# Clustered attention and two MLPs on one core: the times that order its instructions are replaced

## The chip, the cores and the metric

The kernel runs on one core of a Trainium2 chip. The metric is the device time of one execution in microseconds (us). Of the kernel before, three runs were timed, and one more execution was profiled.

## The reference

Attention in which a query sees only the keys of its own cluster (batch 2, 8 heads, 768 tokens, head size 64, 16 centroids a head), then two MLPs on the 1536 tokens. All data is fp32.

```python
q_assign = argmax(einsum('bhsd,hcd->bhsc', q_n, c_n), axis=-1)   # q_n, k_n, c_n: rows divided by their norm
k_assign = argmax(einsum('bhsd,hcd->bhsc', k_n, c_n), axis=-1)
mask = q_assign[:, :, :, None] == k_assign[:, :, None, :]
scores = where(mask, q @ k.T / sqrt(D), -1e9)
attn = exp(scores - max(scores)); attn = attn / (sum(attn) + 1e-9)
x = (attn @ v)                       # to (1536 tokens, 512)
h = x @ w_in;  x = (h * cos(h)) @ w_out               # MLP 1, 512 -> 2048 -> 512
h = x @ w_in2; x = where(h > 0, h, exp(min(h, 0)) - 1) @ w_out2   # MLP 2
```

## The kernel before

**Arithmetic.** TensorE (PE) takes fp32 operands rounded to a shorter form. So each operand is split into a high part and a low part (value minus high part), and a product is made of two or three matmuls. Splitting is work for the other engines: ScalarE (ACT), VectorE (DVE) and GpSimd (POOL).

**Attention.** It handles the 16 heads of the batch in 8 pairs. Each pair has 12 steps, a step being 128 query rows of one head against all 768 keys; 96 steps in all. For a pair, the rows of q and k are transposed (raw_pe, in two halves each), split (raw_out, raw_copy, raw_low) and put together by six DMAs into the stacks X0, X1, T0, T1 (stack). The sums of squares give norms (square, sum_sq, seed, norm_step, norms). The products with the centroids (sims_pe, 12 matmuls for k and 12 for q; X0 serves the pair's first head, X1 its second) are added, scaled, and their first largest gives the cluster of a token (sims_add, sims_scale, sims_max, sims_eq, sims_first, best, assign). The result M is transposed (mask_pe) and copied by mask_out as extra rows into T0 and T1, so that a matmul of the T stacks puts the mask into the scores. The first pair is set up by functions of its own (first_pe, first_hi, first_low, first_hi2), for each of its heads (j = 0, 1) apart.

A step is: qk (L741 with the X stacks, L744 with the T stacks), rowmax (DVE, L749), expo (ACT, L757, the exponential), turn (PE, L766, six transposes in two halves), p_hi (ACT, L780) and p_lo (DVE, L786). Three steps are a half, for which av (L797) makes 12 matmuls with the values; two halves are a unit, one head of one batch. A unit's denominators are turned into reciprocals (recip), written to DRAM and read back spread over the partitions (recip_rows, recip_out: the DMAs row<-den and R<-row), and multiplied in by POOL (x_add, x_mul).

**MLPs.** Each MLP m has 3 tiles t of 512 tokens, and for each tile 16 parts f of the inner dimension. For each (m, t, f), g1 (L198) makes 12 matmuls, act in eight parts applies the nonlinearity and splits the result into GH and GL, and g2 (L257) makes 12 more that add into four accumulators. Before a tile, x_hi and x_lo split its tokens into XH and XL (four pairs); after it, finish copies the accumulators out (e = 0 to 3), in MLP 2 to the output by DMA. The weights of a part f come in two DMAs of 512 KB (load_w), and are converted by w_part: 0 on ACT (L133), 1 and 2 on DVE (L135, L137), 4 on ACT (L142), 5 on POOL (L148); 3 does nothing. They stay in their slot for the three tiles. open_mlp issues the loads of the first ten parts of MLP 1, and close_attention, after the last product of attention, opens the memory for the others and issues their loads.

**Order.** All of this is written out as a list of items, each with a time; the list is sorted by time and then issued, so the times give nothing but the order in which each engine, and each DMA queue, gets its instructions. Every engine works off its instructions in that order and waits where data or a buffer isn't there. The times come from seven tables: FIRST (the first pair, j = 0 and j = 1), PAIR (the other pairs; time 0 of pair pp is step 12(pp-1)), STEP (each step), HALF, UNIT, LAST (the end of attention and the start of MLP 1, counted from step 96) and MLP (m = 0, 1; counted for each unit from step 96 + 2.147). One unit of time is one attention step, or one MLP part.

```python
for n in range(NS):
    for name, time in STEP.items():
        fn, own = named(name)
        at(n + time, fn, n, *own)
...
    for time, _, part, args in sorted(items, key=lambda a: a[:2]):
        part(*args)
```

Buffers that matter here: two PSUM buffers for scores, three for transposes and similarities, one for the attention's output; two buffers u for weights in conversion.

Of the kernel before, what the change touches and what calls it, by code (L numbers as in the profile page):

```python
# [54 lines left out]
def kernel(ctx: ExitStack, tc: tile.TileContext, q, k, v, centroids,  # L55
# [225 lines left out]
    with ExitStack() as actx:  # L281
# [726 lines left out]
```

## Time and profile before

| | |
|---|---|
| timed runs, median | 811.31 us |
| lowest and highest of three | 810.27, 811.99 us |
| span of the profiled execution | 806.6 us |
| PE busy | 781.8 us |
| DVE, ACT, POOL busy | 469.1, 490.3, 408.3 us |

The span runs from the first to the last instruction of the profiled execution; this execution has no time of its own, so the span stands beside the median of the timed runs, 4.7 us above it, and what lies around the span is in that difference. "Granted clock" is the share of full speed that TensorE's clock had in a stretch: 1.00 is 2.4 GHz, 0.50 is 1.2 GHz.

### The profile page before, as it was taken

The page shows a single profiled execution, that of the slowest core. Times are in us where ns is not written, and L with a number is a line of the kernel's source. Part 1 is how long each engine was busy: PE and PEld are TensorE (multiplying, and loading weights), DVE is VectorE, ACT ScalarE, POOL GpSimd, SP SyncE. Part 2 cuts the span into 40 slices and gives each one's busy share as a digit, 9 for nine tenths or more (in the row PEclk, how much of TensorE's full clock was granted, in tenths as well). Part 3 has the DMA queues.
Part 4 walks back from the last instruction along what each step waited for, and adds up shares of the span by engine and source line. Part 5 has one row for each costly group of instructions (what it writes and reads, how often), then busy time and mean ns, then how long its engine had stood idle before and what let it go on. Part 6 is the DMA issues. An engine that isn't in the chain of part 4 may idle for free.

```text
span 806.6 us, 11273 instructions
## 1 busy us (share of the span) xinstructions
PE 781.8 (97%) x4003; PEld 668.4 (83%) x4003; DVE 469.1 (58%) x751; ACT 490.3 (61%) x894; POOL 408.3 (51%) x426
## 2 busy tenths in 40 slices
PE   4999999999998998999999999999999999999997
PEld 3899999999997776888888888888888888888886
DVE  7899899899899768863432443577774111121110
ACT  3798998998999966654433453566563433343332
POOL 3657667667655777652221132379997221122221
PEclk7799999999999999999999999999999999999999
DMA  3645746746637394000000045571000100010001
GB/s 100 141 102 124 181 97 134 167 99 148 161 73 245 52 380 162 1 0 1 1 1 0 1 156 198 176 253 52 1 1 1 52 1 1 0 40 14 0 1 52
DMA packets 62920, 67.99 MB, mean 84 GB/s; under 512 B 30416, under 2 KB 51408, under 8 KB 62864
## 3 DMA queue, kind: packets, MB, share of 16 engines
q1 hardware_dynamic: 62864, 67.28, 30.2%
q8 instruction: 31, 0.51, 0.3%
q14 instruction: 25, 0.20, 0.1%
HBM read 46.17 MB, written 3.19 MB: 61 GB/s over the span
## 4 chain that ended last, share of the span: by engine, by line
PE 82%; DVE 8%; ACT 3%; DMA 3%; POOL 1%; issue 1%; SPq 0%; ACTq 0%; DVEq 0%; POOLq 0%
PE a L257 30%; PE h L198 29%; PE pt L766 6%; PE px L797 6%; PE s L741 3%; PE s L744 3%; PE pt_sim L581 2%; DVE m L749 2%; DMA raw<-in_moe_w_out_dram 2%; PE pt_raw L437 1%; DVE PL L786 1%; POOL slot L148 1%; ACT u L133 1%; DVE u L137 1%; DVE M L647 1%
## 5 line engine op out<-in xcount | busy, mean ns | idle before, releaser
L240 POOL TENSOR_TENSOR GL<-A,GH 128x512 fp32r<-128x512 f32 x96 | 132.1, 1376 | 273.4 <-ACT GH L235 269.4
L198 PE MATMUL h<-XH,slot 128*128 128x512 f32 x768 | 251.9, 391 | 4.4 <-POOL slot L148 4.2
L198 PEld LDWEIGHTS h<-XH,slot 128*128 128x128 f32 x768 | 144.7, 189 | 36.1 <-POOL slot L148 5.6
L198 PE MATMUL h<-XL,slot 128*128 128x512 f32 x384 | 150.1, 391 | 0.0
L232 DVE SCALAR_TENSOR_TENSOR A<-R,h 128x512 f32<-128x512 f32 x48 | 33.0, 687 | 161.3 <-ACT R L230 151.0
L257 PE MATMUL a<-GH,slot 128*128 128x512 f32 x384 | 124.9, 389 | 0.0
L257 PE MATMUL a<-slot,GH 128*128 128x512 f32 x384 | 118.3, 389 | 0.0
L786 DVE TENSOR_TENSOR PL<-pt,PH 128x384 fp32r<-128x384 f32 x192 | 98.3, 543 | 19.4 <-ACT PH L780 17.8
L235 ACT ACTIVATE GH<-A 128x512 fp32r<-128x512 f32 x80 | 50.5, 632 | 76.5 <-DVE A L226 43.1
L780 ACT ACTIVATE PH<-pt 128x384 fp32r<-128x384 f32 x192 | 86.0, 495 | 11.4 <-PE pt L766 9.8
L749 DVE TENSOR_REDUCE m<-s 128x1 f32<-128x768 f32 x96 | 91.0, 948 | 3.1 <-PE s L744 1.8
L766 PE MATMUL pt<-ident,P 128*128 128x128 f32 x576 | 89.5, 280 | 1.4 <-DVE PL L786 1.2
L757 ACT ACTIVATE P<-s,m 128x768 f32<-128x768 f32 x96 | 87.2, 908 | 3.5 <-DVE m L749 3.1
L148 POOL TENSOR_TENSOR slot<-u,slot 128x1024 fp32r<-128x1024 f32 x32 | 79.7, 2492 | 12.8 <-ACT slot L142 12.6
L198 PEld LDWEIGHTS h<-XL,slot 128*128 128x128 f32 x384 | 72.4, 189 | 15.0
L257 PEld LDWEIGHTS a<-slot,GH 128*128 128x128 f32 x384 | 72.1, 188 | 15.0
L257 PEld LDWEIGHTS a<-GH,slot 128*128 128x128 f32 x384 | 72.0, 188 | 15.0
L766 PEld LDWEIGHTS pt<-ident,P 128*128 128x128 f32 x576 | 66.9, 141 | 12.6 <-DVE PL L786 6.4
L257 PE MATMUL a<-GL,slot 128*128 128x512 f32 x192 | 74.7, 389 | 0.0
L257 PE MATMUL a<-slot,GL 128*128 128x512 f32 x192 | 74.7, 389 | 0.0
L219 DVE SCALAR_TENSOR_TENSOR R<-A,h 128x512 f32<-128x512 f32 x48 | 32.9, 686 | 68.4 <-ACT A L215 68.4
L228 ACT ACTIVATE R<-h 128x512 f32<-128x512 f32 x48 | 28.5, 595 | 66.0 <-PE h L198 65.2
(139 smaller groups left out, 1276.9 us busy)
## 6 DMA issues: line engine op xcount, KB each, us to landing
raw<-in_moe_w_in_dram SPq DMA_DIRECT2D x32, 512.0 KB, 5.4
raw<-in_moe_w_out_dram SPq DMA_DIRECT2D x32, 512.0 KB, 6.5
nat_k<-in_k_dram SPq DMA_DIRECT2D x16, 192.0 KB, 4.3
nat_q<-in_q_dram SPq DMA_DIRECT2D x16, 192.0 KB, 3.9
nat_v<-in_v_dram SPq DMA_DIRECT2D x8, 384.0 KB, 3.6
R<-row SPq DMA_DIRECT2D x32, 96.0 KB, 3.4
out_dram<-o SPq DMA_DIRECT2D x12, 256.0 KB, 2.0
X0k<-hi SPq DMA_DIRECT2D x7, 192.0 KB, 2.6
```

The costliest lines, as they stand in the source:

```text
L148: eng.tensor_tensor(out=lo, in0=f32(w_u[m, f]), in1=f32(hi), op=ALU.subtract)
L198: nc.tensor.matmul(h, lhsT=a[:, kd, :], rhs=b, start=(kd == 0 and i == 0), stop=(kd == NKD - 1 and i == 2))
L232: nc.vector.scalar_tensor_tensor(out=A, in0=R, scalar=-1.0, in1=h, op0=ALU.add, op1=ALU.max)
L235: nc.scalar.activation(out=GH, in_=A, func=AF.Copy)
L240: eng.tensor_tensor(out=GL, in0=A, in1=f32(GH), op=ALU.subtract)
L257: nc.tensor.matmul(accs[m, t][e], lhsT=a, rhs=b, start=(f == 0 and i == 0), stop=(f == NF - 1 and i == 2))
L749: nc.vector.tensor_reduce(out=m, in_=st[n]["s"][:, :, 0:HW], axis=AX.XY, op=ALU.max, negate=True)
L757: nc.scalar.activation(out=P, in_=st[n]["s"][:, :, 0:HW], func=AF.Exp, bias=st[n]["m"], accum_out=dens[u][:, j, r:r + 1])
L766: nc.tensor.transpose(pt[:, c * 128:(c + 1) * 128], st[n]["P"][:, e, c * 128:(c + 1) * 128], ident)
L780: nc.scalar.activation(out=ph, in_=pt, func=AF.Copy)
L786: nc.vector.tensor_tensor(out=pl, in0=pt, in1=f32(ph), op=ALU.subtract)
L797: nc.tensor.matmul(tx[g][:, 0:HW], lhsT=V2s[pp][:, j, c, :], rhs=halves[g][a][:, c, :], start=(n == 0), stop=(n == 2 * C - 1))
```

## The change

The seven tables get other numbers. No function, no instruction, no buffer and no choice of engine is changed, and BASE stays 2.147; each engine has the same instructions in another order. The full tables are some 450 numbers; the entries that bear on the order around the opening, the keys' similarities, the av products, the change-over to the MLP and the ends of the tiles are these.

```diff
-FIRST = ({... 'mask_pe': -4.01798, 'mask_out:k': -1.754631, 'mask_out:q': -2.715055},
-  {'first_hi:k': -6.163385, 'first_hi2:k': -4.095755, 'first_low:k': -3.88111, 'first_low:q': -1.740567, 'first_hi2:q': -0.204062,
-   'sims_pe:k': -1.308999, 'sims_pe:q': 0.268773, 'sims_add:k': 0.722591, 'sims_scale': 1.092376, 'assign': 3.113711, 'mask_pe': 3.346959 ...})
+FIRST = ({... 'mask_pe': -7.3245, 'mask_out:k': -4.618, 'mask_out:q': -1.344},
+  {'first_hi:k': -27.1265, 'first_hi2:k': -26.4955, 'first_low:k': -26.5849, 'first_low:q': -39.3125, 'first_hi2:q': -45.6012,
+   'sims_pe:k': -11.2298, 'sims_pe:q': -11.089, 'sims_add:k': -5.6567, 'sims_scale': -4.7338, 'assign': 0.0315, 'mask_pe': 0.3042 ...})
...
-PAIR = {... 'raw_pe:k:1': 0.025604, 'stack:k': 1.900208, 'stack:q': 3.6443, 'load_nat:q': 1.096009, 'load_nat:v': -1.887999,
-  'sims_pe:k:7': 3.547059, 'sims_pe:k:6': 3.591015, ... 'sims_pe:k:5': 4.175453 ...}
+PAIR = {... 'raw_pe:k:1': 0.2089, 'stack:k': 2.1453, 'stack:q': 5.1167, 'load_nat:q': -2.0847, 'load_nat:v': 2.1455,
+  'sims_pe:k:1': 3.133, 'sims_pe:k:8': 3.1663, ... 'sims_pe:k:11': 5.282 ...}
...
-STEP = {'qk': -0.554281, 'rowmax': 0.318128, 'expo': 1.03429, 'turn:0': 1.783177, 'p_hi:0': 2.226495, 'p_lo:0': 2.784921, ...}
+STEP = {'qk': -0.2199, 'rowmax': 0.274, 'expo': 1.1941, 'turn:0': 2.2429, 'p_hi:0': 2.556, 'p_lo:0': 2.7986, ...}
-HALF = {'av:0:0': 5.403758, ... 'av:2:1': 4.964283, ...}
+HALF = {'av:0:0': 5.4843, ... 'av:2:1': 7.6553, ...}
-UNIT = {... 'recip_rows': 7.427179, 'x_mul': 13.848315}
+UNIT = {... 'recip_rows': 8.0355, 'x_mul': 15.1918}
-LAST = {'open_mlp': (-10.431815,), ...
-  'g1': (-0.307886, 1.731051, 4.372541, 5.094428), 'act:3': (6.073842, ..., 8.863032), 'g2': (6.668914, 8.520482, 9.303291, 9.815031),
-  'w_part:5': (5.381259, 5.610103, 6.550675, 6.924254, 7.503784, 8.022706),
-  'w_part:7': (9.14231, 9.347017, 9.526266, 9.904052, 10.071843, 10.148753), ...}
+LAST = {'open_mlp': (-12.9648,), ...
+  'g1': (0.1691, 2.4243, 3.6755, 4.8629), 'act:3': (5.6602, ..., 8.5703), 'g2': (7.6343, 9.1684, 9.5095, 9.8494),
+  'w_part:5': (5.543, 5.6643, 5.7277, 6.1291, 6.3037, 7.7047),
+  'w_part:7': (6.9143, 7.2499, 7.6194, 7.9283, 8.6967, 9.1755), ...}
...
-MLP = ({'g1': 1.795143, 'g2': 5.151129, 'late_g2:13': -0.690981, 'late_g2:14': -1.391747, 'late_g2:15': -0.882423 ...},
-  {'g1': 0.285498, 'g2': 4.282268, 'finish:0': 4.212529, 'finish:1': 4.739817, 'finish:2': 5.863002, 'finish:3': 5.213858 ...})
+MLP = ({'g1': 1.3754, 'g2': 4.3988, 'late_g2:13': -0.2473, 'late_g2:14': 0.1408, 'late_g2:15': -0.1717 ...},
+  {'g1': 0.168, 'g2': 4.6275, 'finish:0': 4.753, 'finish:1': 5.2414, 'finish:2': 5.2833, 'finish:3': 6.8395 ...})
```

PE's order in the change-over, read off the sorted lists: before g1(3), g2(0), g1(4), g2(1), g1(5), g2(2), g2(3), g1(6), g1(7), g2(4), g1(8); after g1(3), g1(4), g2(0), g1(5), g2(1), g2(2), g1(6), g2(3), g1(7), g2(4), g1(8).

## Rows read from the trace of the kernel before

**Rows 1.** The page: busy lines, and the chain that ended last by engine.
```profile
PE 781.8 (97%) x4003; PEld 668.4 (83%) x4003; DVE 469.1 (58%) x751; ACT 490.3 (61%) x894; POOL 408.3 (51%) x426
...
PE 82%; DVE 8%; ACT 3%; DMA 3%; POOL 1%; issue 1%; SPq 0%; ACTq 0%; DVEq 0%; POOLq 0%
```

**Rows 2.** Windows by stage: stretch, its length, busy us (instructions), granted clock, DMA share, GB/s.
```profile
0.00:40.00 40.00, 28.12 (x155) 24.91 (x155) 31.21 (x81) 23.12 (x44) 20.38 (x58) 0.79 0.49 119
40.00:225.00 185.00, 184.25 (x1268) 170.38 (x1267) 166.13 (x321) 169.82 (x387) 126.22 (x196) 1.00 0.60 135
225.00:278.00 53.00, 49.62 (x305) 44.47 (x306) 49.05 (x85) 50.32 (x101) 30.73 (x25) 1.00 0.43 120
278.00:315.00 37.00, 32.69 (x135) 25.91 (x135) 25.00 (x30) 25.44 (x34) 28.27 (x16) 0.95 0.93 316
315.00:802.30 487.30, 487.10 (x2148) 402.69 (x2146) 197.66 (x238) 220.55 (x331) 202.68 (x132) 1.00 0.12 40
```
The busy columns are PE, PE's weight loads, DVE, ACT, POOL.

**Rows 3.** The chain, in order of time: start us, us, what.
```profile
70.58 1.02 PE pt_sim L581 x10
...
101.27 1.02 PE pt_sim L581 x10
...
356.16 8.16 PE a L257 x36
```

**Rows 4.** Timeline of DVE, opening: start, us, line, operation, tiles [idle before].
```profile
17.99 0.36 DVE L647 TENSOR_TENSOR M<-desc,best 128x192 bf16<-128x192 f32 x1
18.38 0.95 DVE L511 SCALAR_TENSOR_TENSOR X1k<-s_raw,T1k 64x768 fp32r<-64x768 f32 x1
...
22.46 0.96 DVE L749 TENSOR_REDUCE m<-s 128x1 f32<-128x768 f32 x1 [1.19 <-PE s L744]
```

**Rows 5.** Timeline of PE, opening.
```profile
11.42 1.46 PE L581 MATMUL pt_sim<-CC,X0k 128*128 128x32 f32 x6 [2.21 <-ACT X0k L518]
...
18.40 0.82 PE L655 MATMUL pt_mask<-identb,M 128*128 128x128 bf16 x6 [2.91 <-DVE M L647]
```

**Rows 6.** Windows of the instructions on tile sm: DVE, POOL, clock, DMA.
```profile
22.00:32.00 10.00, 3.95 (x7) 0.00 (x0) 0.68 0.48 118
```

**Rows 7.** Windows of 2 us, all engines; columns as in rows 2.
```profile
26.00:28.00 2.00, 2.00 (x10) 1.90 (x10) 1.97 (x4) 0.64 (x1) 1.92 (x3) 0.50 0.18 41
28.00:30.00 2.00, 1.46 (x9) 1.14 (x8) 1.97 (x4) 1.87 (x6) 1.59 (x3) 0.90 0.94 230
...
308.00:310.00 2.00, 1.99 (x5) 1.62 (x6) 1.97 (x3) 2.00 (x3) 2.00 (x2) 0.58 1.07 369
```

**Rows 8.** Timeline of PE, the last pair's setup.
```profile
208.44 0.55 PE L437 MATMUL pt_raw<-ident,nat_k 128*128 128x128 f32 x3
...
217.09 0.47 PE L581 MATMUL pt_sim<-CC,X1k 128*128 128x32 f32 x3
```

**Rows 9.** Timeline of SP's DMA queue, the last pair's setup: time of issue.
```profile
212.17 0.59 SPq L477 DMA_DIRECT2D X1k<-lo  x1
```

**Rows 10.** Tile X1k between 190 and 225: its two DMAs.
```profile
DMA to landing us min/median/max: 3.0/3.9/4.8
```

**Rows 11.** Timeline of PE, change-over to the MLP.
```profile
278.00 0.39 PE L198 MATMUL h<-XH,slot 128*128 128x512 f32 x1
...
294.00 0.72 PE L198 MATMUL h<-XH,slot 128*128 128x512 f32 x2 [1.76 <-POOL slot L148]
...
308.01 0.99 PE L198 MATMUL h<-XH,slot 128*128 128x512 f32 x2 [2.39 <-POOL slot L148]
...
314.75 0.39 PE L198 MATMUL h<-XH,slot 128*128 128x512 f32 x1
```

**Rows 12.** Timeline of all engines, 284 to 294: the conversions of part 5.
```profile
284.73 1.13 ACT L133 ACTIVATE u<-raw 128x1024 f32<-128x1024 f32 x1 [0.94 <-DMA raw<-in_moe_w_out_dram]
...
291.22 2.72 POOL L148 TENSOR_TENSOR slot<-u,slot 128x1024 fp32r<-128x1024 f32 x1
```

**Rows 13.** Timeline of ACT, the end.
```profile
802.27 1.08 ACT L274 ACTIVATE o<-a 128x512 f32<-128x512 f32 x2 [0.71 <-PE a L257]
```

More of the change, by code (lines that the diff above doesn't have):

```diff
@@ L28 @@
-STEP = {'qk': -0.554281, 'rowmax': 0.318128, 'expo': 1.03429, 'turn:0': 1.783177, 'p_hi:0': 2.226495, 'p_lo:0': 2.784921, 'turn:1': 1.918261, 'p_hi:1': 2.322276, 'p_lo:1': 2.867829}
-HALF = {'av:0:0': 5.403758, 'av:0:1': 6.750175, 'av:1:0': 7.350891, 'av:1:1': 6.901501, 'av:2:0': 5.134225, 'av:2:1': 4.964283, 'av:3:0': 5.242615, 'av:3:1': 5.420227, 'av:4:0': 7.325687, 'av:4:1': 7.204538, 'av:5:0': 6.486225, 'av:5:1': 5.404756, 'x_main': 7.995152, 'x_low': 7.577939}
-UNIT = {'den_eps': 3.395449, 'recip': 4.382076, 'recip_rows': 7.427179, 'recip_out': 8.211055, 'x_add': 9.795484, 'x_mul': 13.848315}
@@ new lines @@
+PAIR = {'raw_pe:k:0': -0.743, 'raw_out:k:0': -0.2045, 'raw_low:k:0': 0.6817, 'raw_pe:k:1': 0.2089, 'raw_out:k:1': 0.4515, 'raw_low:k:1': 0.6139, 'stack:k': 2.1453, 'raw_pe:q:0': 1.5546, 'raw_out:q:0': 1.7927, 'raw_low:q:0': 3.1418, 'raw_pe:q:1': 2.3762, 'raw_out:q:1': 3.0458, 'raw_low:q:1': 4.0128, 'stack:q': 5.1167, 'square:k': 1.3021, 'square:q': 1.3101, 'sum_sq:k': 3.1266, 'sum_sq:q': 3.5134, 'sims_add:k': 5.7012, 'seed': 4.0682, 'sims_add:q': 7.1365, 'norms': 6.4333, 'sims_scale': 7.5265, 'sims_max': 7.7243, 'sims_first': 8.322, 'load_nat:k': -9.4917, 'load_nat:q': -2.0847, 'load_nat:v': 2.1455, 'raw_copy:k:0': -0.1846, 'raw_copy:k:1': -0.967, 'raw_copy:q:0': 1.7891, 'raw_copy:q:1': 3.107, 'best': 8.3585, 'sims_eq': 7.8239, 'values_hi:0': 5.6735, 'values_lo:0': 6.6448, 'values_hi:1': 9.3594, 'values_lo:1': 9.4649, 'norm_step:0': 4.1104, 'norm_step:1': 5.1523, 'norm_step:2': 6.1592, 'norm_step:3': 6.3018, 'sims_pe:k:0': 3.1708, 'sims_pe:k:1': 3.133, 'sims_pe:k:2': 5.0754, 'sims_pe:k:3': 3.3276, 'sims_pe:k:4': 3.491, 'sims_pe:k:5': 4.5188, 'sims_pe:k:6': 3.2098, 'sims_pe:k:7': 3.2376, 'sims_pe:k:8': 3.1663, 'sims_pe:k:9': 3.7707, 'sims_pe:k:10': 3.9263, 'sims_pe:k:11': 5.282, 'sims_pe:q:0': 6.7398, 'sims_pe:q:1': 6.6346, 'sims_pe:q:2': 6.079, 'sims_pe:q:3': 6.0556, 'sims_pe:q:4': 6.4121, 'sims_pe:q:5': 6.2837, 'sims_pe:q:6': 6.4203, 'sims_pe:q:7': 6.4759, 'sims_pe:q:8': 6.474, 'sims_pe:q:9': 6.435, 'sims_pe:q:10': 6.6393, 'sims_pe:q:11': 6.7459, 'assign': 8.771, 'mask_pe': 9.0336, 'mask_out': 9.3553}
@@ new lines @@
+STEP = {'qk': -0.2199, 'rowmax': 0.274, 'expo': 1.1941, 'turn:0': 2.2429, 'p_hi:0': 2.556, 'p_lo:0': 2.7986, 'turn:1': 2.3257, 'p_hi:1': 2.6658, 'p_lo:1': 2.8786}
+HALF = {'av:0:0': 5.4843, 'av:0:1': 5.5958, 'av:1:0': 5.4825, 'av:1:1': 7.7439, 'av:2:0': 7.6152, 'av:2:1': 7.6553, 'av:3:0': 6.8609, 'av:3:1': 6.0871, 'av:4:0': 5.5957, 'av:4:1': 7.241, 'av:5:0': 7.2689, 'av:5:1': 5.6122, 'x_main': 7.873, 'x_low': 7.8732}
+UNIT = {'den_eps': 4.4246, 'recip': 4.4277, 'recip_rows': 8.0355, 'recip_out': 8.2123, 'x_add': 12.5024, 'x_mul': 15.1918}
```

7 lines of the change are left out of this document (3 added, 4 removed).

## The prediction

> **What bounds the kernel now.** I read the page's busy lines and its chain first, then the span cut into stages, then each stage by its own timeline. TensorE (PE) is busy 781.8 of 806.6 us, and 82% of the chain that ended last is PE; VectorE (DVE), ScalarE (ACT) and GpSimd (POOL) lie between 51% and 61% [rows 1]. The change leaves every matmul in place, so only PE's 24.8 us of idle time, and the time in which its clock is low, can move. The stages say where that is [rows 2]: 11.9 us in the first 40 us, 0.75 in 185 us of steady attention, 3.4 in the last eighth of attention (225 to 278), 4.3 in the change-over to the MLP (278 to 315), 0.2 in the 487 us after it, and the 4.3 that are left lie behind the last matmul.
>
> Steady attention repeats every 30.69 us (101.27 less 70.58), which is 12 steps of 2.557 us, and the MLP's 12 matmuls of one g1 or g2 take 2.72 us (8.16 for 36) without a gap [rows 3]. Nothing can be gained there; something can be lost, because a matmul that comes up before its data stops PE at once. Gain can come from the opening, the change-over and the tail alone.
>
> **The opening.** Before assigns head 0, starts qk(0), and puts head 1's assignment between the first steps. After puts head 1's splits and similarities ahead of head 0's mask, and head 1's whole assignment ahead of the first row maximum. On DVE three splits of 0.95 us (X1k, and X1q twice) now stand in front of head 0's chain, which ended at 18.35 [rows 4]: 21.2 now. On PE mask_pe(0) is queued behind the sims of both tensors of head 1, up to 1.46 us each at the low clock [rows 5], which can't start before X1k is split. I get mask_pe at about 22.05 against 18.40. From mask_pe to the first row maximum the way is the same but for one of those sims, which stood before qk(0) and no longer does; the row maximum, at 22.46 in before [rows 4], starts some 3.2 us later.
>
> What is given back is head 1's chain, which ran between the row maxima while DVE was full (1.97 of 2 us in both windows of [rows 7]): 3.95 us on the tile of similarities [rows 6] and 0.36 for M [rows 4], 4.3 us. So DVE would be 1.1 us ahead at the sixth row maximum, if it stays the limit. Against that stands the clock. It fell to 0.50 (1.2 GHz) in the 2.21 us in which PE waited for X0k [rows 5], and was back at full (2.4 GHz) between 28 and 30 (0.90 over that window, so at about 28.4 [rows 7]), after PE had run without a gap from 18.40. In after PE waits some 5 us before head 1's sims, and its gapless run starts with mask_pe, 3.65 us later. If the return is as much later, 3.65 us more run at half rate and cost 1.8. Sum: +3.2 - 4.3 + 1.8 = **+0.7 us**. Bounds: -1.1 (the clock costs nothing), +5.0 (nothing is given back).
>
> The Trainium skill, page TensorE: Matmul & The Clock Gate, section Part 1: The HAM clock gate, says that the warm-up is a budget of time and not a number of matmuls. By it the half-rate stretch moves with the late start, and the opening is +0.7; if the return stayed at 28.4 it would be -1.1. The trace agrees in so far as the clock fell in a gap and rose within a dense run.
>
> **Steady attention.** On the three busy engines the step's own parts (qk two ahead, row maximum, exponential, turn, hi and lo copies) keep their order against each other; the av products of a half are dealt 5/1/6 to three steps instead of 6/0/6, which costs PE nothing. The sims of the keys come earlier. Their tables stand 3.55 - 0.03 = 3.52 steps behind raw_pe(k,1) in before and 3.13 - 0.21 = 2.92 in after. In the trace that was 217.09 - 208.44 = 8.65 us [rows 8], so now 7.2. The data of X1k goes by DMA: its last part is issued 3.73 us behind raw_pe [rows 9] and lands 3.0 to 4.8 us later [rows 10], so it is there 6.7 to 8.5 us behind raw_pe. The first X1k chunk comes some 0.3 us into the sims. The slack is then +0.8 to -1.0 us, where before had 0.1 or more. PE idles 0.12 us in a period (0.75 in six [rows 2]), so a wait isn't hidden by anything. Taking most pairs near the short landing I put **+0.5** for all; bounds 0 and +6 (1.0 in six pairs). The later stack and loads of q have more than a step of room.
>
> **End of attention.** The first ten weight DMAs are issued 1 us sooner, as one pair of denominator DMAs no longer stands before them; as many conversions as before stand ahead of step 96 on ACT, which is the limit there in both orders (50.3 of 53 us busy, DVE 49.1 [rows 2]): **0**. Bounds -1.1 and +1.1, one first conversion (1.13 us [rows 12]) in a better or worse place.
>
> **The change-over.** From g1(2) at 278.00 to g1(8) at 314.75 PE does 11 groups of 12 matmuls, 29.9 us by 2.72; it took 36.75, so 6.8 us are lost [rows 11]: 2.1 in g1(5), which waits 1.76 us for POOL's last conversion w5(5), and most of the rest in g1(7), 2.39 us of waiting for w5(7) and then matmuls at a granted clock of 0.58 [rows 7]. After moves the conversions of units 6 and 7 on ACT and DVE forward against the activations of units 3 to 5, so w5(6) and w5(7) go ahead; but it also takes one g2 out from before g1(5), which comes up 2.72 us earlier, at 288.9. Its third matmul (289.35) needs w5(5). That chain of five conversions started at 284.73 with the landing and ended at 293.94 [rows 12]: 9.2 us, of which 6.8 are work (the first 1.13, the last 2.72, 2.97 between them) and the rest waits. The last reciprocal comes some 0.4 us earlier, so the landing is at 284.3 and the end between 291.1 and 293.5. After has fewer items between the five, so I take 291.7, nearer the work alone. The stall is then 2.4 us, which is that of 308.01, and what followed that one was the slow stretch: ten matmuls took 3.98 us (308.01 to 311.99) where ten take 2.27, 1.7 lost. Unit 6's w5 then ends about 296.5 and is due about 299.5, unit 7's about 300.3 against 304.9: a w5 of 2.7 and a GL of 1.3 take POOL 4 us a unit and PE takes 5.44, so no second stall. Loss 2.4 + 1.7 = 4.1 in place of 6.8: **-2.7**. Bounds: with the end at 291.1 and the clock kept, as it was behind the 1.76 us (the matmuls after it were not longer), a loss of 1.8 and -5.0; with the end at 293.5 and the slow stretch, 4.2 + 1.7 and -0.9; with a second stall like the first, +1.2.
>
> **MLP and tail.** Where a tile of tokens changes, three g2 (8.16 us [rows 3]) cover the splits XH and XL; after leaves two in MLP 1 (5.44) and one in MLP 2 (2.72). Walking the splits by their durations I find the last XL of MLP 1 ready 6.4 to 7.6 us after the accumulators' end where it is needed at 7.7, and the tightest XL of MLP 2 at 3.9 against 4.3. **+0.2**, bounds 0 and +1.5. In the tail two output copies, 1.08 us together [rows 13], follow the last matmul, because the third output is queued behind the fourth; after has them in order, so one copy goes: **-0.5**, bounds 0 and -0.5.
>
> **Sum.** 0.7 + 0.5 + 0 - 2.7 + 0.2 - 0.5 = -1.8 us: a span of 804.8 for 806.6. The median of the three timed runs, 811.31, is 4.7 above this span, and I carry that over: **809.5 us**.
>
> **Rivals.**
> 1. *The late opening isn't made up* (slower). Place: the first row maximum. If ACT or the stack DMAs, and not DVE, hold the steps that follow, head 1's 4.3 us give nothing back and +5.0 stands for +0.7: 813.8. For it: ACT was 1.87 of 2 us busy at 28 to 30 [rows 7] and has the same work left. Against: DVE was fuller. It decides from an opening that is 4.1 us late (0.7, the 1.8 of gain, and 1.6 to be seen).
> 2. *The change-over gains almost nothing.* The chain of w5(5) keeps its 9.2 us and stops PE sooner instead of later: -0.9 for -2.7, 811.3.
> 3. *The keys' sims wait for their DMA* in each pair, 1.0 us in six: +6 for +0.5, 815.0. For it: PE has no idle time to hide it; against: landings of 4.8 us are the longest.
> 4. *The splits at the tile changes come late*, 1.0 us at each of five: +5 for +0.2, 814.3.
>
> **Chances.** Forecast 0.50, rivals 0.20, 0.16, 0.09 and 0.05. A measurement can tell about 0.2% (1.6 us) from no change. The forecast's own range is 805.5 to 811; of its half 0.44 lies over 1.6 us faster (a change-over without the slow stretch, 807.8, adds to it) and 0.06 within. Rival 2 gives 0.14 within and 0.02 slower, rival 1 0.03 and 0.17; 3 and 4 are slower. Faster 0.44, same 0.23, slower 0.33. The range runs from the forecast's lower end to a little over rival 1: 805.0 to 814.5.
>
> **What would show it.** Opening: the first row maximum at about 25.6, full clock at about 32, and the period marks of [rows 3] 0.7 us later. Steady: a period of 30.69 to 30.8; a wait of pt_sim on the DMAs of X1k would be rival 3. Change-over: one stall, at g1(5), of 2 to 2.5 us, none at g1(7). Tile changes: no gap. Tail: one copy behind the last matmul. The prediction is wrong if the marks come 3 us late, or if g1(6) or g1(7) stalls again.

## The result, and the profile after

After took 815.92 us in the median of seven runs (812.45 to 820.9), before 810.87 (810.11 to 811.99): a ratio of 1.0061, 95% interval 1.0034 to 1.0088. The change made the kernel 5 us slower, where 809.5 and "faster" were forecast, and the median lies outside the forecast range of 805.0 to 814.5; rival 3 had stood at 815.0. The runs of after also lie 8.5 us apart, those of before 1.9. The profiled execution of after took 813.07 us with a span of 811.3, so it is one of its quicker ones, and 1.8 us lie around the span. One execution in this document, the profiled one of the reverse experiment (848.65 us), is slow against the others of its kernel and stands in no median.

The page of after, busy lines and chain, as in [rows 1]:

```profile
PE 779.9 (96%) x4003; PEld 668.2 (82%) x4003; DVE 496.8 (61%) x751; ACT 487.4 (60%) x894; POOL 411.0 (51%) x426
...
PE 72%; DVE 11%; ACT 7%; DMA 5%; POOL 2%; issue 2%; SPq 1%; ACTq 0%; POOLq 0%; DVEq 0%
```

DMA went from 3% to 5% of the chain and PE from 82% to 72%. The same windows as in [rows 2], columns as there:

```profile
0.00:40.00 40.00, 26.30 (x141) 23.09 (x142) 28.83 (x80) 23.05 (x41) 19.94 (x56) 0.74 0.53 124
40.00:225.00 185.00, 177.72 (x1228) 165.18 (x1227) 161.44 (x310) 164.97 (x375) 121.41 (x183) 1.00 0.56 127
225.00:278.00 53.00, 50.58 (x328) 45.99 (x326) 49.75 (x88) 50.64 (x107) 31.84 (x39) 1.00 0.50 140
278.00:315.00 37.00, 33.20 (x143) 27.55 (x143) 29.08 (x36) 27.92 (x38) 25.14 (x14) 0.95 0.83 271
```

PE's idle time between 40 and 225 us was 0.75 us and is 7.3. A fixed window holds other work in a kernel that runs late, so the ledger is made from marks: the start of the n-th row maximum (DVE, L749) in each timeline. The columns after the first are us behind before at the same row maximum, called the lag below; "loads moved" and "FIRST alone" are experiments of the next section.

| row maximum of step | before, start | after | loads moved | FIRST alone |
|---|---|---|---|---|
| 0 | 22.46 | +3.55 | +3.38 | +3.50 |
| 12 | 54.60 | +1.46 | +1.29 | +1.59 |
| 48 | 146.66 | +5.21 | +0.38 | +1.91 |
| 84 | 238.28 | +7.25 | +0.37 | +1.67 |

The last matmul ended at 802.25 in before and at 807.51 in after (+5.3), the span at 806.6 and 811.3 (+4.7). So the opening cost 1.5 us, steady attention 5.8 (7.25 less 1.46), the rest won back 2.0 up to the last matmul and 0.6 behind it.

What PE waited for in after between 40 and 240 us (releaser: us in total, times, longest):

```profile
PE pt_mask L655 <- DVE M L647: 2.3, 7, 0.7
PE pt_sim L581 <- DMA X1k<-lo: 2.0, 2, 1.4
PE pt_sim L581 <- DMA X1q<-lo: 1.7, 4, 0.5
PE pt_sim L581 <- DMA X0q<-lo: 1.2, 2, 0.7
```

4.9 us are similarities that wait for DMAs of a stack, 2.9 of them for the stack of q, and 2.3 are the mask's transposes. None of these lines was there in before between 40 and 240. The chain of after runs through the same DMAs; the period, which was 30.69 us [rows 3], is 33.2 here (106.50 less 73.29), in the longest of the six periods:

```profile
67.89 5.26 DMA X1q<-lo
73.29 1.03 PE pt_sim L581 x8
92.46 4.17 DMA X1k<-lo
...
101.11 5.26 DMA X1q<-lo
106.50 1.04 PE pt_sim L581 x8
```

The timeline of the DMA queue, one pair later, shows what is new: the loads of v and k, with the denominators' DMAs between and behind them, now stand between the stack of k and the stack of q. In before both loads came after the stack of q or with the mask's DMAs.

```profile
93.78 0.62 SPq L479 DMA_DIRECT2D T1k<-hi  x1
94.45 0.59 SPq L311 DMA_DIRECT2D nat_v<-in_v_dram  x1
95.09 1.31 SPq L823 DMA_DIRECT2D R<-row  x2
96.44 1.29 SPq L317 DMA_DIRECT2D nat_k<-in_k_dram  x2
97.83 1.33 SPq L817 DMA_DIRECT2D row<-den  x2
99.26 0.51 SPq L474 DMA_DIRECT2D X0q<-hi  x1
```

Opening. PE waited 5.64 us before head 1's similarities and reached mask_pe at 22.00 (22.05 was forecast, 18.40 in [rows 5]):

```profile
19.41 1.46 PE L581 MATMUL pt_sim<-CC,X1k 128*128 128x32 f32 x6 [5.64 <-ACT X1k L518]
...
22.00 0.82 PE L655 MATMUL pt_mask<-identb,M 128*128 128x128 bf16 x6
```

The first row maximum started at 26.01 (25.6 was forecast). The granted clock was 0.65 over 30 to 32 us, so full from about 31.4 (28.4 in before [rows 7]):

```profile
30.00:32.00 2.00, 2.00 (x11) 1.67 (x10) 0.96 (x1) 1.95 (x6) 1.92 (x3) 0.65 1.00 257
```

End of attention. A new stall: on DVE the conversion L137 of weight part 3 (3.28 us beside POOL's L148) stands ahead of a split PL, and PE's turn waits 2.35 us for it. Timelines of DVE and of PE, then windows:

```profile
276.73 3.28 DVE L137 SCALAR_TENSOR_TENSOR u<-raw,u 128x1024 uint32<-128x1024 uint32 x1
279.93 1.01 DVE L786 TENSOR_TENSOR PL<-pt,PH 128x384 fp32r<-128x384 f32 x2
```

```profile
280.53 0.90 PE L766 MATMUL pt<-ident,P 128*128 128x128 f32 x3 [2.35 <-DVE PL L786]
...
300.83 0.72 PE L198 MATMUL h<-XH,slot 128*128 128x512 f32 x2 [1.45 <-POOL slot L148]
...
320.57 0.73 PE L198 MATMUL h<-XH,slot 128*128 128x512 f32 x2 [0.39 <-POOL slot L148]
```

```profile
280.00:282.00 2.00, 1.47 (x6) 1.47 (x7) 1.97 (x7) 1.90 (x4) 0.76 (x1) 0.64 0.04 8
282.00:284.00 2.00, 2.00 (x7) 1.61 (x6) 2.00 (x4) 1.96 (x3) 1.63 (x1) 0.51 0.08 2
```

Behind this wait the granted clock fell to 0.51, as it did to 0.58 behind the 2.39 us of [rows 11]. The change-over itself has two stalls left, 1.45 us at g1(5) and 0.39 at g1(8). From the last av at 290.59 to g1(8) at 319.57 PE does 10 groups of 12 matmuls, 27.2 us of work in 28.98: 1.8 us lost, where before lost 6.8 up to the same place; 2.5 with the 0.7 that g1(8) itself loses. Tail: all four copies run in order, and one of 0.6 us is left behind the last matmul (ACT; two in [rows 13]):

```profile
805.50 2.64 ACT L274 ACTIVATE o<-a 128x512 f32<-128x512 f32 x4 [5.71 <-PE a L257]
```

### The profile page after: what moved, and what is told of

It reads as the page before. It is cut to its first block, busy times and chain, and to the rows that moved or that the text cites. A ratio compares the mean times of both kernels' runs of the same rounds, so it can differ in the third digit from the quotient of the medians.

```text
span 811.3 us, 11271 instructions
## 1 busy us (share of the span) xinstructions
PE 779.9 (96%) x4003; PEld 668.2 (82%) x4003; DVE 496.8 (61%) x751; ACT 487.4 (60%) x894; POOL 411.0 (51%) x426
## 4 chain that ended last, share of the span: by engine, by line
PE 72%; DVE 11%; ACT 7%; DMA 5%; POOL 2%; issue 2%; SPq 1%; ACTq 0%; POOLq 0%; DVEq 0%
PE a L257 31%; PE h L198 30%; PE pt L766 3%; DVE m L749 3%; DVE PL L786 3%; PE px L797 3%; DMA X1q<-lo 3%; ACT P L757 2%; PE s L741 2%; PE s L744 2%; PE pt_sim L581 2%; ACT PH L780 1%; DMA X1k<-lo 1%; DVE u L137 1%; DMA raw<-in_moe_w_out_dram 1%
## 5 line engine op out<-in xcount | busy, mean ns | idle before, releaser
L240 POOL TENSOR_TENSOR GL<-A,GH 128x512 fp32r<-128x512 f32 x96 | 136.6, 1423 | 261.5 <-ACT GH L235 243.7
L749 DVE TENSOR_REDUCE m<-s 128x1 f32<-128x768 f32 x96 | 91.3, 951 | 4.7 <-PE s L744 4.2
L148 POOL TENSOR_TENSOR slot<-u,slot 128x1024 fp32r<-128x1024 f32 x32 | 81.5, 2548 | 23.4 <-ACT slot L142 22.9
L766 PEld LDWEIGHTS pt<-ident,P 128*128 128x128 f32 x576 | 68.6, 142 | 10.5 <-DVE PL L786 5.5
L137 DVE SCALAR_TENSOR_TENSOR u<-raw,u 128x1024 uint32<-128x1024 uint32 x32 | 67.9, 2121 | 0.4
L215 ACT ACTIVATE A<-h,cbias 128x512 f32<-128x512 f32 x48 | 32.9, 684 | 53.2 <-PE h L198 52.7
```

The lines of the kernel that those rows point to most:

```text
L137: nc.vector.scalar_tensor_tensor(out=u, in0=low, scalar=29, in1=u, op0=ALU.logical_shift_right, op1=ALU.bitwise_or)
L148: eng.tensor_tensor(out=lo, in0=f32(w_u[m, f]), in1=f32(hi), op=ALU.subtract)
L240: eng.tensor_tensor(out=GL, in0=A, in1=f32(GH), op=ALU.subtract)
L749: nc.vector.tensor_reduce(out=m, in_=st[n]["s"][:, :, 0:HW], axis=AX.XY, op=ALU.max, negate=True)
L766: nc.tensor.transpose(pt[:, c * 128:(c + 1) * 128], st[n]["P"][:, e, c * 128:(c + 1) * 128], ident)
```

## The experiments

Fifteen kernels ran, with tables mixed or edited, or with DMAs moved or added. Times are medians, with before's median on the same chip beside them.

**One table, or the loads alone.** The first kernel takes the whole table PAIR back:

```diff
-PAIR = (after's)
+PAIR = (before's)
```

> The kernel after with one table, PAIR, taken back from before. In the trace of after the row maxima fall behind those of before by 1.46 us up to step 12 and by 7.25 us at step 84, so 5.8 us are lost in the setups of the six later pairs. Theory PAIR (the order of the setup's DMAs, sims and masks against each other): this comes back whole, the lag at step 84 is about 1.5 us and the time about 810 us. Rival STEP/HALF (the step's own order or the spread of the av products takes the time): the lag at step 84 stays over 5 us and the time stays near 816 us.

846.2 us (before 810.2; ratio 1.0443, 1.0424 to 1.0462). Neither theory: the lag at step 84 is 37.5 us. Before's setup doesn't fit between after's steps: PE waits for splits, masks and raw transposes that come at another place in the step. A table can't be judged by swapping it whole. The second moves two loads:

```diff
-PAIR = {... 'load_nat:k': -9.4917, ..., 'load_nat:v': 2.1455, ...}
+PAIR = {... 'load_nat:k': -6.8, ..., 'load_nat:v': -1.9, ...}
```

> The kernel after with two entries of PAIR changed: the loads of k and v are put behind the stack of q on SP's queue (load_nat:k -6.8, load_nat:v -1.9) in place of between the two stacks. Theory queue: the 2.9 us in which TensorE waits for X0q and X1q vanish, and some of the 2.0 us for X1k, since the loads no longer share the DMA engines with the stacks; about 812 us, the mask's waits of 0.25 us a pair stay. Rival sims: the similarities of q and k come up too early whatever lies in the queue; the waits stay within 1 us of 4.9 and the time near 816 us.

807.15 us (before 810.17; 0.9961, 0.9948 to 0.9975): 8.8 us less than after, and faster than before. The lag at step 84 goes from 7.25 to 0.37. PE's waits between 40 and 245 us:

```profile
PE pt_mask L655 <- DVE M L647: 2.3, 7, 0.7
PE pt_sim L581 <- DMA X1q<-lo: 0.4, 1, 0.4
```

The waits for X1k and X0q are gone, those for the mask stay. So two numbers hold the whole loss, of 350 (the seven tables have 350 numbers, not some 450). From step 12 to 84 this kernel even gains 0.9 us on before. Windows from the row maximum of step 24 to that of step 72, first of before, then of the loads moved, columns as in [rows 2]:

```profile
85.29:208.30 123.01, 122.55 (x842) 113.25 (x840) 110.33 (x214) 112.81 (x257) 85.59 (x133) 1.00 0.61 137
86.29:208.28 121.99, 120.59 (x842) 113.27 (x841) 109.68 (x213) 113.17 (x257) 85.55 (x132) 1.00 0.61 137
```

The same 842 matmuls keep PE busy 2.0 us less in these four periods, at the same clock. So after's order does gain something in steady attention, and its two loads hid it; which entries of the tables give the gain was not tried. The spans of the two profiled executions are 4.6 us apart (811.3 and 806.7), the medians 8.8: after's profiled execution lies 2.9 us below its median, this one's (808.44) 1.3 above its own. What else the median execution of after waits for can't be read from these two traces. Each of the two alone:

```diff
-'load_nat:v': 2.1455
+'load_nat:v': -1.9
```

> The kernel after with one number changed: load_nat:v -1.9, so that the load of v goes to SP's queue behind the mask's DMAs, and no longer right behind the stack of k; the load of k stays ahead of the stack of q. Moving both loads took 8.8 us off (807.15 for 815.92). Theory: the two loads are alike in what they do to the stack of q (0.6 us of SP's queue for one DMA of 384 KB, 1.3 us for two of 192 KB; the same bytes on the DMA engines), and waits of TensorE appear only where both add up beyond the slack of about 1 us; so each move alone gives more than half of the 8.8: 809 to 811 us. Rival: the loss comes from one of them, v (it lies between the two stacks and competes with X1k's landing too): this run 807, the run with k alone moved 815.

```diff
-'load_nat:k': -9.4917
+'load_nat:k': -6.8
```

> The kernel after with one number changed: load_nat:k -6.8, so that the load of k goes behind the stack of q; the load of v stays behind the stack of k. Theory: as for v alone, 809 to 811 us. Rival v: 815 us, as nothing changes for X1k. Rival k (1.3 us of queue time just ahead of the stack of q is the larger part): 807 us here, 814 with v alone moved.

807.98 (before 810.47; 0.9969, 0.9958 to 0.9981) and 808.97 (0.9983, 0.9971 to 0.9996). Either move takes away most of the loss, v 7.9 and k 7.0 of 8.8 us, even more than the theory said. So most of the loss needs both loads; with only k moved PE still waits 2.1 us for X1k, behind whose DMAs the load of v stands, with only v moved 0.6 for X1k and 0.9 for X1q.

**The reverse.** The same two numbers put into before:

```diff
-PAIR = {... 'load_nat:k': -7.620661, ..., 'load_nat:v': -1.887999, ...}   (before's)
+PAIR = {... 'load_nat:k': -9.4917, ..., 'load_nat:v': 2.1455, ...}
```

> The reverse of moving the loads back: the kernel before with two numbers of PAIR taken from after (load_nat:k -9.4917, load_nat:v 2.1455), so that the loads of v and k stand between the stack of k and the stack of q. In before the last parts of the stack of q land about 1.1 us ahead of the first similarity that reads them (65.38 + 3.2 = 68.6 against 69.70 for X1q). In after the loads cost the stack of q 1.7 to 2 us in the queue and 1.2 us in landing. Theory: about 3 us less 1.1 of slack, 1 to 2 us of waiting in each of six pairs, most of it X0q and X1q: 6 to 12 us slower, 817 to 822. Rival: the loss in after needs its other shifts too (the earlier similarities of k, the later stack of q); here 812 us or less.

836.2 us (median of five, 831.25 to 842.44; before 810.9; 1.0321, 1.0282 to 1.0360): some 25 us lost, three times the 8.8 that the same two numbers cost in after, and more than the theory gave. Two things in the traces go that way; neither was tried by itself. Before reads the stack sooner: in the pair of steps 12 to 23 X1q is first read 13.7 us behind the issue of the first DMA of the stack of k (69.70 less 56.03), with the loads moved 14.8 (72.10 less 57.35). And the clock falls: in the profiled execution (the one of 848.65 us) PE waits 13.1 us for X0q in five pairs, up to 3.1 at a time, and the granted clock between 40 and 225 us is 0.90 in the mean, where it is 1.00 in before and in after. A mean of 0.90 is half rate for a fifth of 185 us, some 18 us lost by this estimate:

```profile
PE pt_sim L581 <- DMA X0q<-lo: 13.1, 5, 3.1
...
40.00:225.00 185.00, 170.76 (x1053) 157.99 (x1053) 140.91 (x266) 141.14 (x320) 104.66 (x163) 0.90 0.50 113
```

**Issued late, or landing late.** Loads on another engine's queue:

```diff
-nc.sync.dma_start(out=t, in_=src[b, 2 * hp:2 * hp + 2]...)             # v
-nc.sync.dma_start(out=nats[pp, which][:, j], ...)                       # k and q
+(nc.gpsimd if pp > 1 else nc.sync).dma_start(out=t, ...)
+(nc.gpsimd if pp > 1 and which == "k" else nc.sync).dma_start(out=nats[pp, which][:, j], ...)
```

> The kernel after with its tables as they are, but with the loads of v and k of pairs 2 to 7 issued by GpSimd's queue in place of SP's, at the same place in the list. The bytes still go over the DMA engines beside the stacks; the stacks no longer stand behind the loads in SP's queue. Theory place in the queue: the stack of q is issued earlier again and TensorE's waits for it shrink to under 1.5 us of 4.9; 807 to 809 us. Rival shared DMA engines: X1q still takes 4.6 us to land in the median (3.4 with the loads moved away), the waits stay over 3 us; 813 us or more. GpSimd's own time for the issues is within its idle half.

837.6 us (before 810.05; 1.0334, 1.0299 to 1.0370). X1q lands in 6.3 us in the median. The rival's direction, but not a clean test: GpSimd's stream also changed, and X0q<-lo was issued 3.9 us behind X0q<-hi (0.6 in after), as its split on POOL came late: POOL issued the loads just ahead of it, which took 0.76 and 1.66 us. The Trainium skill, page DMA: Bandwidth & Descriptors, section Issuing engines are not separate DMA queues, says that issuing from several engines saves only the time of the issue. The trace agrees in that the landing got no shorter (6.3 us for 4.6). So next comes queue time without the loads' bytes, in the kernel with the loads moved: three small DMAs ahead of the stack of q, as below, and then six.

```diff
+def idle_dmas(pp):
+    for i in range(3):
+        d = rows_dram.tile([128, 2], F32, ...)
+        nc.sync.dma_start(out=d, in_=ident[:, 0:2])
 def stack(pp, w):
     need(("lo", pp, w, 0), ("lo", pp, w, 1))
+    if w == "q":
+        idle_dmas(pp)
```

> The kernel with both loads moved (807.15 us) and three extra DMAs of 1 KB (to scratch memory that nobody reads) issued on SP's queue just ahead of each stack of q, in seven pairs. They take the 1.8 us of the queue that the two loads took, and next to no bytes. Theory place in the queue: the stack of q lands 1.8 us later, 4 us or more are lost over the pairs: 811 us or more. Rival shared DMA engines: without the loads' bytes the stack of q lands in its usual 3.3 us and the slack of about 1 us hides most of it: under 809 us.

> The same with six such DMAs a pair, 3.6 us of the queue. Both theories expect a loss here, since 3.6 us are far over the slack: theory place in the queue 820 us or more; rival shared DMA engines 812 to 818, from 2 us over the slack in seven pairs.

827.3 us (before 810.4; 1.0209, 1.0188 to 1.0231) and 883.6 (1.0903, 1.0882 to 1.0924). By the expectation that is place in the queue, but the run doesn't tell the two apart: three DMAs of 1 KB took 1.4 us of the queue, and X1q also landed in 6.1 us where 3.4 is usual. They had 128 rows of 8 bytes each, and the stack behind them landed late. Here too the clock fell behind the longer waits: 0.96 in the mean between 40 and 225 us with three of them, 0.84 with six. The same with one row of 512 bytes:

```diff
-    for i in range(3):
-        d = rows_dram.tile([128, 2], F32, ...)
-        nc.sync.dma_start(out=d, in_=ident[:, 0:2])
+    for i in range(4):
+        d = rows_dram.tile([1, 128], F32, ...)
+        nc.sync.dma_start(out=d, in_=ident[0:1, :])
```

> As with the three extra DMAs of 128 rows of 8 bytes, which took 1.4 us of SP's queue but also let X1q land in 6.1 us in place of 3.4: now four extra DMAs a pair of one row of 512 bytes each, ahead of the stack of q, in the kernel with both loads moved. They take about 1.7 us of the queue, and one packet each on the DMA engines. Theory place in the queue: the time stays well over the 807 us of the kernel without them, 811 or more, with X1q landing in about 3.4 us. Rival DMA engines: landing and time come back to 807 to 809 us, and the 827 us were the small packets' time on the DMA engines.

807.96 us (before 810.35; 0.9968, 0.9956 to 0.9981), as without them. The four take 1.55 us of the queue, and X0q<-hi is issued behind them, but PE waits only 0.2 us for X1q. The queue's timeline, then PE's waits between 40 and 245 (lines of kernel.py are 7 higher here, so L588 is L581):

```profile
94.72 1.55 SPq L471 DMA_DIRECT2D idle<-ident  x4
96.36 0.48 SPq L481 DMA_DIRECT2D X0q<-hi  x1
...
98.17 0.59 SPq L484 DMA_DIRECT2D X1q<-lo  x1
```

```profile
PE pt_sim L588 <- DMA X1q<-lo: 0.2, 1, 0.2
```

This is less than it seems, for the stack's last part was not 1.55 us late. Without the four, in the same pair, the queue stands idle for 1.0 us ahead of X0q<-lo, which waits for its split, and the four fill that gap:

```profile
94.38 0.48 SPq L474 DMA_DIRECT2D X0q<-hi  x1
95.86 0.48 SPq L475 DMA_DIRECT2D X0q<-lo  x1
...
97.04 0.59 SPq L477 DMA_DIRECT2D X1q<-lo  x1
```

Counted from the issue of the pair's X0k<-hi, X1q<-lo is issued after 9.3 us in five of the six pairs behind 45 us with the loads moved, after 9.6 to 10.5 with the four, after 9.8 to 11.4 with three DMAs of 8-byte rows, and after 10.0 to 12.2 in after (in the pair with 12.2, 1.4 of it arose before the loads, as X0k<-lo had to wait for POOL). The sixth pair, where one issue takes some 3 us, has 11.9 and 11.8 in the first two. So a delay of 0.3 to 1.2 us cost nothing measurable. The landing of the two main parts of the stack X1q in these six pairs, from the tile's view (us, minimum, median, maximum), in this order: after, loads moved, three DMAs of 8-byte rows; the view gives none for the four of one row.

```profile
DMA to landing us min/median/max: 3.4/4.6/5.6
```

```profile
DMA to landing us min/median/max: 3.0/3.4/5.2
```

```profile
DMA to landing us min/median/max: 4.7/6.1/8.1
```

The two small-DMA kernels put the stack at much the same place in the queue, and the one with 8-byte rows loses 20 us: there a longer landing goes with the loss. In after both things are there, an issue up to 2.9 us later and a landing 1.2 us longer in the median. That the two loads between the stacks cause the loss is shown; how much of it comes from the place in the queue and how much from the landing is not.

**The opening by itself.**

```diff
-FIRST = (before's)
+FIRST = (after's)
```

> The kernel before with FIRST alone taken from after: the opening by itself. Theory: the lag of 1.5 us at step 12 is carried to the end, since steady attention has no idle time in which to win it back: 812.4 us against 810.9. Rival: it is made up later (end of attention or change-over, where engines wait anyway), 810.9 us within 0.5.

811.51 us (before 810.17; 1.0016, 1.0003 to 1.0028): +1.3, and the lag of 1.6 us stands unchanged from step 12 to step 84. Steady attention gives nothing back.

**End of attention and change-over by themselves.**

```diff
-UNIT, LAST, MLP = (before's)
+UNIT, LAST, MLP = (after's)
```

> The kernel before with UNIT, LAST and MLP taken from after: end of attention, change-over, MLPs and tail by themselves. Theory: these win what after wins between step 84 (7.25 us behind) and the last matmul (4.7 behind), and a copy less in the tail: 2.6 to 3.1 us, 808 us. Rival: the conversions of LAST stand where after's steps need them, and between before's steps they stop TensorE longer than in after (2.35 us at the turn of step 94, then the low clock): 811 us or more.

833.8 us (before 810.2; 1.0294, 1.0262 to 1.0327), with 20 us lost by step 66. UNIT places the reciprocals' DMAs ahead of the stack of q; X0q<-hi is issued at 65.52 in place of 62.74, and X1q lands in 4.6 us. Without UNIT:

```diff
-LAST, MLP = (before's)
+LAST, MLP = (after's)
```

> The kernel before with LAST and MLP taken from after, UNIT left as in before. With UNIT too it took 833.8 us, and 21 of the 23 us were lost between steps 12 and 66, where no entry of LAST or MLP is; so UNIT lost them, by reciprocals and their DMAs that stand later in SP's queue, ahead of the stacks. Theory: without UNIT the attention runs as in before up to step 84 (lag 0 +- 0.3), and what is left is the gain of the change-over and the tail less the new stall before the turn of step 94: 807 to 809 us. Rival: LAST's conversions disturb before's steps: 811 or more with a lag that grows from step 84 on.

813.1 us (before 810.5; 1.0027, 1.0015 to 1.0038). The lag from step 12 to 84 grows by 0.4 us only (24.5 with UNIT), and the rival holds at the end: after's conversions between before's steps give two new waits, at a qk and at an av:

```profile
263.99 1.01 PE L741 MATMUL s<-X1k,X1q 128*128 128x384 f32 x2 [2.12 <-ACT P L757]
...
280.83 0.69 PE L797 MATMUL px<-PL,V 128*128 128x384 f32 x1 [3.17 <-ACT X L850]
```

So the change-over can't be measured apart from its steps; its gain is read from the trace of after alone.

**The new stall, and what holds the change-over.** From the kernel with the loads moved:

```diff
-'w_part:3': (-0.3075, 0.1888, 0.3896, 1.3338, 1.3716, 2.123)
+'w_part:3': (-0.3075, 0.1888, 0.95, 1.72, 1.75, 2.123)
```

> The kernel with both loads moved (807.15 us), and the second VectorE conversion of weight part 3, with ScalarE's that follows it, put behind step 94's split of P. In after and in that kernel this conversion (3.28 us beside GpSimd's) stands ahead of the split, TensorE's turn waits 2.3 us and the clock falls to 0.5 behind it. Theory: the wait and the slow stretch go (2.3 and about 1.7 us), and no more than 1 us comes back at g1(5), which stalls anyway: 803 to 805 us. Rival: the wait only moves to g1(5), which is then reached earlier while its weights land no sooner, since their DMAs start when attention closes: 806.5 to 807.5 us.

807.08 us (before 810.47; 0.9960, 0.9945 to 0.9976): the rival. The turn's wait shrank from 2.3 to 0.6 us. There was no slow stretch to win back: the clock had fallen behind this wait in after, but with the loads moved it stayed at 1.00 behind 2.29 us, so that part of the expectation was a misreading. PE and window of the kernel with the loads moved:

```profile
273.60 0.55 PE L766 MATMUL pt<-ident,P 128*128 128x128 f32 x3 [2.29 <-DVE PL L786]
...
274.00:276.00 2.00, 2.00 (x12) 1.74 (x11) 1.97 (x7) 2.00 (x4) 1.69 (x1) 1.00 0.20 14
```

And g1(5) got its weights at 291.8 in both kernels and waited much as long (1.36 and 1.76 us there), here:

```profile
291.79 0.50 PE L198 MATMUL h<-XH,slot 128*128 128x512 f32 x1 [1.18 <-ACT slot L142]
...
294.28 1.22 PE L198 MATMUL h<-XH,slot 128*128 128x512 f32 x2 [1.75 <-POOL slot L148]
```

The loads of the next weights were issued at 279.50 here and at 281.16 with the stall left in, yet ACT's first conversion of part 5, which waits for its weights to land, began at 287.48 here and at 287.47 there. Why the earlier issue brought no earlier landing is open. (This profiled execution was also 1.0 us later at step 84, with a lag of 1.41 us for 0.37; the medians are equal.) With the second g2 put back ahead of g1(5):

```diff
-'g2': (7.6343, 9.1684, 9.5095, 9.8494)
+'g2': (7.6343, 8.45, 9.5095, 9.8494)
```

> The kernel with both loads moved and part 3's conversion behind step 94's split (807.08 us), and in the change-over the second g2 put back ahead of g1(5), as in before. There TensorE waits 1.2 and 1.75 us in g1(5) and its clock falls to 0.5; GL of unit 1 is ready at 287.0 and g2 of unit 0 ends at 290.5, so the second g2 can run at once and cover 2.72 us. Theory: 2.7 us of waiting and most of the slow stretch (1 us) go: 803 to 804.5 us. Rival: the weights come at the pace of their DMAs, so g1(6) and g1(7), due as early as before, wait in place of g1(5): 806.5 to 807.5 us.

806.55 us (before 810.05; 0.9950, 0.9931 to 0.9969): the rival again, at its lower edge. g1(5)'s waits shrink to 0.77 us, and g1(8) waits in their place, with a granted clock of 0.50 behind its wait:

```profile
293.54 0.73 PE L198 MATMUL h<-XH,slot 128*128 128x512 f32 x2 [0.77 <-POOL slot L148]
...
313.21 0.74 PE L198 MATMUL h<-XH,slot 128*128 128x512 f32 x2 [2.54 <-POOL slot L148]
```

This is the lowest median of the study, but 0.5 us from the two kernels before it is within the spread of their runs. Last, the mask's waits:

```diff
-'mask_pe': 9.0336, 'mask_out': 9.3553
+'mask_pe': 9.345, 'mask_out': 9.6
```

> The kernel of the run before this one with the mask's transposes put 0.3 steps later (mask_pe 9.345, mask_out 9.6), behind the turn of their step. In after and all kernels from it TensorE waits 0.25 us in each pair for M. Theory: 1.5 us over six pairs: 1 to 1.5 us under the kernel before it in this list. Rival: the later mask copies delay ScalarE's step in turn, which is as full as TensorE: no difference over 0.5 us.

808.45 us (before 810.05; 0.9982, 0.9970 to 0.9995): 1.9 us slower than without it, so neither theory. PE's waits for M are gone, and 2.1 us of waits of turn for PL stand in their place. In this order the 2.3 us of waits for the mask could not be had; they only moved to another tile.

## Why the prediction was wrong

The step that failed is "steady attention", the term +0.5, and in it the last sentence: "The later stack and loads of q have more than a step of room." The working followed the stack of k, whose landing the trace of before showed at 3.0 to 4.8 us [rows 10], and carried that landing over to a DMA queue whose order had changed. The loads of v and k were not in the sum at all. They were put between the two stacks; the stack of q was then issued up to 2.9 us later and landed in 4.6 us for 3.4, and 5.8 us were lost where +0.5 was written. More than a step of room was there and was not enough: X1q<-lo was issued at 67.89, PE came for it at 72.76 (73.29 less a wait of 0.53), 4.9 us or almost two steps later, and it landed after 5.26 (PE's line here, the DMA's in the chain above):

```profile
73.29 0.59 PE L581 MATMUL pt_sim<-CC,X1q 128*128 128x32 f32 x4 [0.53 <-DMA X1q<-lo]
```

The bounds, 0 and +6, held by luck, since +6 stood for six waits on X1k. Moving the two loads back and putting them into before show the cause from both sides; the shares of queue and landing stay open.

"Nothing can be gained there" failed too, on the other side: with the loads moved, steady attention ran 1.0 us faster over four periods than in before.

- *Rival 3* had the size (+6) and named the wrong tensor: of 4.9 us of waits on stacks 2.9 are X0q's and X1q's, 2.0 X1k's. Without the two loads no wait on X1k is left, so its slack (+0.8 to -1.0) by itself was not the trouble. A chance of 0.09 was too low for a place with no idle time and a changed DMA order.
- *Opening*: right in mechanism, half the size. +0.7 forecast, +1.5 in the trace at step 12, 1.3 in the run with FIRST alone. First row maximum, mask_pe and return of the clock came within 0.6 us of the forecast; full clock came back 3.0 us later than in before for 3.65 forecast. The Trainium skill, page TensorE: Matmul & The Clock Gate, section Part 1: The HAM clock gate, makes the warm-up a matter of time, so that it moves with the late start; the trace agrees with the move, and can't tell time from a number of matmuls, since both orders run much the same ones there.
- *End of attention*: wrong. The equal-work lag goes from 7.25 us at step 84 to 9.9 at the last av: before's 278.00 stands against after's 290.59 less 2.72, as after has done one g1 more. That is +2.6 where 0 with bounds of 1.1 was written. The stall of 2.35 us behind L137 and the low clock after it are the largest loss that the trace shows there; only the counts of conversions ahead of step 96 were compared, and not what stands just ahead of each split. In the kernel with the loads moved, where the clock had not fallen, taking the stall away gained nothing (807.08 for 807.15), since the next weights then held PE at g1(5). In after itself it was not taken away.
- *Change-over*: right in mechanism, and -4.4 (6.8 lost in before, 2.5 in after with g1(8)) for -2.7; up to the start of g1(8), where the forecast ended, it is -5.0, its lower bound. There was one stall at g1(5), of 1.45 us instead of 2.4, and no slow stretch. A late arrival helped: with the loads moved PE comes earlier, and g1(5) waits 1.36 and 1.76 us with a granted clock of 0.50 behind it.
- *MLP*: right, no gap at a tile change. *Tail*: 3.8 us behind the last matmul for 4.35, -0.5 forecast.

The time around the span, 4.7 us carried over, holds 1.8 us in after's profiled execution; the rest is the distance of a quick execution from the median, alike for both kernels (differences of 4.7 in the spans, 5.05 in the medians).

Sum by what was measured in the profiled executions: 1.5 + 5.8 + 2.6 - 4.4 - 0.2 - 0.6 = 4.7, the difference of the spans. The -0.2 of the MLP part is the rest.

## What to carry to other kernels

Where all transfers share one queue, a new order for the engines is also a new order for the DMAs, and the landing time read from an old trace holds only for the old neighbours: list for every transfer on the critical path what is issued in the 5 us ahead of it. In a schedule with next to no idle time waits are paid in full: 4.5 us more of waits on stacks (4.9 and 0.4) went here with 6.7 us more lag between steps 12 and 84. Tables that were made together can't be judged by swapping one of them: four mixes here took 811.5 to 846.2 us, while two single numbers held the whole loss. And a wait that is taken away is a gain only where nothing else is due behind it; look first for what PE meets next.

## What the runs showed of the hardware

Three DMAs of 128 rows of 8 bytes (3 KB in all) ahead of each stack of q let it land 2.7 us later (6.1 for 3.4) and cost 20 us over the kernel, in part through the lower clock behind the waits; four of one row of 512 bytes cost nothing measurable. The Trainium skill, page DMA: Bandwidth & Descriptors, section Specifications, names 512 bytes as the least transfer for full rate; the two runs agree in direction, and no run here tells the number of rows from their size.

The same conversion L137 took 1.22 us in before and 3.28 us in after. First before, then POOL in after just ahead of the line at 276.73 shown above:

```profile
287.70 1.22 DVE L137 SCALAR_TENSOR_TENSOR u<-raw,u 128x1024 uint32<-128x1024 uint32 x1
```

```profile
276.35 2.58 POOL L148 TENSOR_TENSOR slot<-u,slot 128x1024 fp32r<-128x1024 f32 x1 [2.28 <-ACT slot L142]
```

POOL's instruction ended at 278.93, and the conversion 1.08 us later. All 64 conversions of the two profiled executions fall in line. In 34 an instruction of POOL was running at their start, with more than 0.2 us to go; they took 1.60 to 3.37 us and ended 1.07 to 1.10 us behind its end. The other 30 took 1.21 to 1.24 us, 24 of them although an instruction of POOL started within them. So the conversion waits until the running instruction of POOL is over, and one that starts later does not slow it down.

A wait of much the same length was followed by a lower clock in one execution and not in another: 2.35 us in after (0.51 behind it) and 2.29 us with the loads moved (1.00).
